# Sums of a weight's four blocks in a fused attention, MoE and GLU kernel: five adding DMAs and two negated copies against four VectorE subtractions

## The chip, the cores and the metric

The kernel runs on one core of a Trainium2 chip. The metric is the device time of one launch in microseconds, as the median of several runs. The engines are TensorE (PE, with its weight loads shown apart as PEld), VectorE (DVE), ScalarE (ACT), GpSimd (POOL) and SyncE (SP); each works through its own list of instructions in the order in which the program wrote them, and waits where an instruction needs something that another engine or a DMA has not finished.

## What is computed

Block-causal attention, then a mixture of eight experts over its output, then a gated linear unit. Cut to what matters:

```python
attn = softmax(mask(q @ k.T / sqrt(64))) @ v          # 4 x 8 heads, 576 positions
x = attn as (2304, 512)
P = eight rounds of row and column normalising of exp(x @ w_gate)
x = sum over e of P[:, e] * (relu(x @ w1[e]) @ w2[e])  # 8 experts, 512 -> 1024 -> 512
g = x @ w_gate2
y = (g * sigmoid(g) * (x @ w_val)) @ w_out             # 512 -> 1536 -> 512
```

## The kernel before

Every matrix product is done at float32 precision with float16 operands: a float32 matrix is scaled by a power of two and cut into a high and a low float16 half, and a product is three float16 products. On top of that a 512 x 512 weight W is cut into four blocks, W11, W12, W21 and W22, and a product uses seven products of block sums in place of eight (a Strassen-Winograd scheme). A weight therefore has to be turned into seven operands: W11, W21, W22, and the sums T1 = W12 - W11, T3 = W22 - W12, T2 = W22 - T1 and T4 = W21 - T2, up to signs. Each operand takes ACT one instruction for its high half (line 173, `split_later`) and DVE one for its low half (line 174); in the code `up(o, src)` issues the first and `low(o)` the second.

The expert weights come as 16 units of 512 hidden columns, each with two weights (w1 and w2). A unit is 63 slots of work of TensorE: five blocks of tokens (four of 256 columns, one of 128), seven operand products each (`products_in`, line 543), with the second product of the unit before (`products_out`, line 651) woven in. A bank of PSUM that `products_in` has filled must be emptied by ACT (lines 560, 568, 572, 779) or by DVE's adds (lines 565, 574, 580) before TensorE gets it again. While TensorE works through unit u, a background list prepares unit u+1's two weights, and, spread over 13 of the units, converts the three GLU weights from float64 words. `Background.step` takes a task from the list (a light one may bring a first task of the next weight along), at most twice a slot, so as to have the list done by slot 58. The maxima of a weight's blocks (`mx`, line 376) come first, then its scale (`end`), and then `sum_tasks`, lines 284 to 345, which is what the change rewrites. 39 weights go through `sum_tasks`: 30 expert weights and 9 pieces of GLU weights (gate, value and output, three each). A unit during which a GLU piece goes through it has three weights to sum in place of two.

In `sum_tasks` before, the sums are made in place in the float32 blocks b[r][c] by `add`: a DMA issued from POOL's queue with accumulation, SBUF to SBUF, 256 KB. So that adding will do, W12 and W21 have been negated in place by ACT (`minus`, line 348), called from `mx` for the expert weights and from `first` (line 494) for the GLU pieces. The last two of the five adds need the result of an earlier one. The low halves are written in the step after the high half, and three empty steps (`gap`) stand among the tasks.

The names in the profile: `wr` are an expert weight's float32 blocks, `w` its operands; `f_g`, `f_v`, `f_o` the blocks of a GLU piece, `gg`, `gv`, `go` their operands; `abc_m_a`, `abc_m_b`, `abc_m_c` the three PSUM banks of `products_in`; `m_t` sums that are taken out of them; `ev` results of the second product, added into `acc` by another DMA with accumulation from POOL's queue (line 1433).

Of the kernel before, what the change touches and what calls it, by code (L numbers as in the profile page):

```python
# [13 lines left out]
AF = mybir.ActivationFunctionType  # L14
ALU = mybir.AluOpType
# [10 lines left out]
W11, W21, W22, T4, T1, T2, T3 = range(7)  # L26
# [4 lines left out]
def attention_moe_glu_kernel(  # L31
# [21 lines left out]
    nc = tc.nc  # L53
# [166 lines left out]
    places = Places(0)  # L220
# [63 lines left out]
    def sum_tasks(b, sp, name, flip):  # L284

        los = {}

        def add(o, x):
            nc.gpsimd.dma_start(o, x, accum_op=ALU.add)  # L292

        def up(o, src, minus=False):
            los[o] = sp(o, src, minus)

        def low(o, *gone):
            los.pop(o)()
            places.give(*gone)

        def t0():
            up(W11, b[0][0])

        def t1():
            low(W11)
            add(b[0][0], b[0][1])
            up(W21, b[1][0], True)

        def t2():
            low(W21)  # L310
            add(b[1][0], b[1][1])
            up(W22, b[1][1])

        def t3():
            low(W22)
            add(b[0][1], b[1][1])

        def t5():
            up(T1, b[0][0], True)
            add(b[1][0], b[0][0])  # L320

        def t6():
            low(T1)
            add(b[1][1], b[0][0])

        def t8():
            up(T3, b[0][1])

        def t9():
            low(T3, b[0][1])  # L330
            up(T4, b[1][0], True)
            places.give(b[0][0])

        def t10():
            low(T4, b[1][0])
            up(T2, b[1][1], flip)

        gap = (0, None, 0)
        return (
            [(1, t0, 0), (1, t1), (1, t2), (0, t3)]  # L340
            + [gap] * 1
            + [(1, t5, 0), (0, t6)]
            + [gap] * 2
            + [(1, t8, 0), (1, t9), (1, t10), (0, lambda: low(T2, b[1][1]))]
        )

    def minus(x):
        nc.scalar.activation(x, x, AF.Copy, scale=-1.0)

    units, made = {}, set()  # L350

    def expert_items(u):
# [8 lines left out]
        for i, W in enumerate((W1, W2)):  # L361
            g = {"b": [[None, None], [None, None]]}
# [9 lines left out]
                        nc.sync.dma_start(b, src.rearrange("(k p) f -> p k f", p=P))  # L372
                g["mx"] = small.tile([P, 4], F32, tag="wmx", name=f"wmx_{u}_{i}")

            def mx(k, g=g, sums=i == 0 or u >= 2):
                nc.vector.tensor_reduce(
                    g["mx"][:, k : k + 1], g["b"][k // 2][k % 2], axis=AX.XY, op=ALU.max, apply_absolute_value=True
                )
                if sums and k > 1:
                    minus(g["b"][(k - 1) // 2][(k - 1) % 2])  # L380

            def begin(g=g, i=i):
                m1 = small.tile([P, 1], F32, tag="wm1", name=f"wm1_{u}_{i}")
# [35 lines left out]
    def glu_items(name, src, rawp):  # L419
# [5 lines left out]
        g = {}  # L425
# [11 lines left out]
        def mx(b, r, c):  # L437
            k = 2 * r + c
            if k == 0:
                g["mx"] = small.tile([P, 4], F32, tag="wmx", name=f"gmx_{name}")  # L440
            nc.vector.tensor_reduce(
                g["mx"][:, k : k + 1], b[r][c], axis=AX.XY, op=ALU.max, apply_absolute_value=True
            )
# [14 lines left out]
        def exponent(cur, b, t, r, c):  # L458
            b[r][c] = places.take(f"f_{name}_{t}_{r}{c}", F32, main=False)
            cur["f"] = b[r][c].rearrange("p k w -> p (k w)")  # L460
            nc.scalar.activation(cur["f"], cur["high"], AF.Copy, scale=2.0**-112)

        def shift(cur):
            fi = cur["f"].bitcast(I32)
            nc.vector.tensor_single_scalar(fi, fi, 3, op=ALU.logical_shift_left)

        def sign(cur):
            fi, hi = cur["f"].bitcast(I32), cur["high"].bitcast(I32)
            nc.vector.scalar_tensor_tensor(fi, hi, -(2**31), fi, op0=ALU.bitwise_and, op1=ALU.bitwise_or)
# [16 lines left out]
        for t, r, c in quads:  # L486
            if (r, c) == (0, 0):
                b = [[None, None], [None, None]]
            cur = {}

            def last(cur=cur, b=b, r=r, c=c):
                mx(b, r, c)

            def first(cur=cur, b=b, q=(t, r, c)):
                exponent(cur, b, *q)
                if q[1:] == (1, 0):
                    minus(b[0][1])
                elif q[1:] == (1, 1):
                    minus(b[1][0])

            tasks = [(1, first, 0)]
            tasks += [(0, lambda cur=cur: (shift(cur), sign(cur))), (0, lambda cur=cur: mantissa(cur)), (0, last, 2)]
            if (r, c) == (1, 1):
                tasks[-1] = (0, lambda last=last, t=t: (last(), begin(t)))
                tasks += [(0, None, 0), (lambda force: across_made(g["r"])(force), lambda t=t: end(t))]
                tasks += sum_tasks(b, lambda o, src, minus=False, t=t: sp(t, o, src, minus), f"g{name}_{t}", name == "o")
            items.append((0, lambda cur=cur, q=(t, r, c): load(cur, *q), tasks))
# [1237 lines left out]
```

## Time and profile before

| | |
|---|---|
| median of 3 runs | 2194.89 us (2191.09 to 2196.18) |
| the profiled execution | 2203.99 us, span 2202.2 us |
| adds of line 292 | 195 of 256 KB |
| adds of line 1433 | 351 of 256 KB |

The profiled execution lies 0.4% above the median of the other runs. Its stages: attention, with the first two units beside it, up to about 390 us; the units up to about 1790 us; then the GLU. Views are read like this. A row of a table by stretch gives the stretch, its length, then busy microseconds of PE, PEld, DVE, ACT and POOL with the number of instructions, the granted TensorE clock (1.00 is 2.4 GHz, 0.5 is 1.2 GHz), the share of time in which DMA engines were busy, and GB/s; the stretches here run from one unit's first weighting on DVE (line 1412) to the next unit's. A row of waits gives who waited for whom, the sum in us, how often, and the longest. A row of the order of time gives the start, the length, the engine, what it did, and in brackets how long the engine had been idle and what ended that. A row of instructions by line ends with count, busy us and the mean in ns.

### The profile page before, as it was taken

To read this page: it belongs to the slowest core of one execution; us is meant where nothing else is said; L and a number is where in the kernel's file an instruction comes from. 1 tells how busy PE (TensorE), PEld (TensorE's weight loads), DVE (VectorE), ACT (ScalarE), POOL (GpSimd) and SP (SyncE) were. 2 spreads that over 40 slices of the span, in tenths; PEclk is the share of its full clock that TensorE was granted. 3 is DMA by queue.
4 is the path that set the end of the run, shared out by engine and by line. 5 is a ranking of instruction groups with operands and counts; after the bars stand their busy time and mean duration, and the time that the engine had idled before them with its cause. 6 is when DMAs were issued, how large, how long until landed. Compare 5 with 4: busy or idle time off the path is not lost.

```text
span 2202.2 us, 47643 instructions
## 1 busy us (share of the span) xinstructions
PE 2001.1 (91%) x18378; PEld 1696.4 (77%) x18378; DVE 1596.5 (72%) x3583; ACT 1366.3 (62%) x2901; POOL 708.0 (32%) x1003
## 2 busy tenths in 40 slices
PE   6789899799989999898998988999888988999997
PEld 3356667688877888777887877888777887888887
DVE  6887774677777787776876767777776787666766
ACT  5666665467676677666776666677666556544442
POOL 4544343203333343333433333343333122100000
PEclk8889999899999999999999999999999999999999
DMA  6343331527887888878888797878879110210211
GB/s 170 104 121 96 106 88 48 148 54 149 173 183 151 171 158 171 185 144 174 157 167 178 145 182 146 176 148 161 186 146 202 40 45 1 57 46 17 62 40 49
DMA packets 180787, 272.22 MB, mean 124 GB/s; under 512 B 18512, under 2 KB 72784, under 8 KB 180560
## 3 DMA queue, kind: packets, MB, share of 16 engines
q0 software_dynamic: 78624, 143.17, 38.5%
q1 hardware_dynamic: 101936, 126.01, 18.7%
q8 instruction: 144, 2.36, 0.4%
q14 instruction: 83, 0.68, 0.1%
HBM read 90.98 MB, written 24.38 MB: 52 GB/s over the span
## 4 chain that ended last, share of the span: by engine, by line
PE 38%; DMA 17%; DVE 12%; issue 8%; ACT 6%; POOL 2%; POOLq 0%; ACTq 0%; DVEq 0%; SPq 0%
DMA wr<-wr 9%; PE abc_m_b L543 7%; PE m_o_b L651 6%; PE m_o_ac L651 5%; PE abc_m_c L543 3%; PE abc_v_b L543 3%; PE m_go_b L651 3%; PE abc_g_b L543 3%; PE m_go_ac L651 2%; PE abc_m_a L543 2%; DMA f_v<-f_v 2%; DMA f_g<-f_g 2%; DVE m_t L710 1%; DVE m_h L183 1%; PE abc_v_c L543 1%
## 5 line engine op out<-in xcount | busy, mean ns | idle before, releaser
L543 PEld LDWEIGHTS <-w 128*128 128x128 f16 x6720 | 620.0, 100 | 185.0 <-issue 111.4
L651 PEld LDWEIGHTS <-m_h 128*128 128x128 f16 x5292 | 521.0, 99 | 77.2 <-issue 11.6
L543 PE MATMUL abc_m_b<-xs,w 128*128 128x256 f16 (+1 forms) x3840 | 490.7, 269 | 71.5 <-DVE m_t L565 33.0
L1433 POOL DMA_DIRECT2D acc<-ev x351 | 340.4, 1098 | 549.7 <-ACT ev L1440 447.9
L651 PE MATMUL m_o_b<-w,m_h 128*128 128x256 f16 x3024 | 407.1, 274 | 5.9 <-ACT ev L1440 5.6
L651 PE MATMUL m_o_ac<-w,m_h 128*128 128x256 f16 x2268 | 320.7, 279 | 3.1 <-ACT ev L1440 3.1
L543 PE MATMUL abc_m_c<-xs,w 128*128 128x256 f16 (+1 forms) x1920 | 235.7, 267 | 22.9 <-ACT m_r L779 21.0
L173 ACT ACTIVATE w<-wr,ws 128x512 f16<-128x512 f32 x210 | 149.4, 720 | 123.1 <-DMA wr<-wr 109.0
L174 DVE SCALAR_TENSOR_TENSOR w<-wr,ws,w 128x512 f16<-128x512 f32 x210 | 156.9, 752 | 94.4 <-ACT w L173 94.1
L292 POOL DMA_DIRECT2D wr<-wr x150 | 147.5, 990 | 228.1 <-DMA wr<-wr 57.2
L1440 ACT ACTIVATE ev<-m_o_b,pe 128x256 f32<-128x256 f32 x351 | 161.6, 475 | 58.1 <-PE m_o_b L651 53.1
L183 DVE TENSOR_TENSOR m_h<-m_t,m_h 128x512 f16<-128x512 f32 (+1 forms) x210 | 132.9, 634 | 35.0 <-ACT m_h L689 34.8
L1440 ACT ACTIVATE ev<-m_o_ac,pe 128x256 f32<-128x256 f32 (+1 forms) x234 | 134.3, 579 | 36.9 <-PE m_o_ac L651 35.8
L682 ACT ACTIVATE m_h<-m_t 128x512 f16<-128x512 f32 (+1 forms) x210 | 120.5, 582 | 36.1 <-DVE m_t L580 18.5
L689 ACT CAST m_h<-m_t 128x512 f16<-128x512 f32 (+1 forms) x210 | 122.0, 581 | 16.7 <-DVE m_t L710 16.4
L686 DVE SCALAR_TENSOR_TENSOR m_h<-m_t,m_h 128x512 f16<-128x512 f32 (+1 forms) x210 | 131.1, 633 | 1.1 <-ACT m_h L682 0.7
L543 PEld LDWEIGHTS <-gg_w 128*128 128x128 f16 x1260 | 114.2, 98 | 21.4 <-issue 9.3
L1002 POOL TENSOR_SCALAR e<-e,r 128x64 f32<-128x64 f32 (+2 forms) x144 | 78.9, 555 | 159.8 <-DVE r L997 100.6
L651 PEld LDWEIGHTS <-g_h 128*128 128x128 f16 x1134 | 111.8, 99 | 19.6 <-issue 5.4
L543 PEld LDWEIGHTS <-gv_w 128*128 128x128 f16 x1260 | 114.4, 98 | 13.3 <-issue 1.2
L543 PE MATMUL abc_m_a<-xs,w 128*128 128x256 f16 (+1 forms) x960 | 119.3, 265 | 0.0
L691 POOL TENSOR_TENSOR g_h<-g_t,g_h 128x512 f16<-128x512 f32 (+1 forms) x15 | 16.0, 1069 | 250.8 <-ACT g_h L689 250.8
(319 smaller groups left out, 3454.8 us busy)
## 6 DMA issues: line engine op xcount, KB each, us to landing
acc<-ev POOLq DMA_DIRECT2D x351, 256.0 KB, 5.3
wr<-wr POOLq DMA_DIRECT2D x150, 256.0 KB, 4.0
wr<-in_w_dram SPq DMA_DIRECT2D x128, 256.0 KB, 4.7
st<-hl SPq DMA_DIRECT2D x48, 144.0 KB, 3.6
raw_g<-in_w_gate_dram SPq DMA_DIRECT2D x12, 512.0 KB, 5.1
raw_v<-in_w_val_dram SPq DMA_DIRECT2D x12, 512.0 KB, 5.4
raw_o<-in_w_out_dram SPq DMA_DIRECT2D x12, 512.0 KB, 4.8
scr_g<-gg SPq DMA_DIRECT2D x21, 256.0 KB, 3.6
```

The lines of the kernel that those rows point to most:

```text
L173: nc.scalar.activation(hi, src, AF.Copy, scale=s)
L174: return lambda: nc.vector.scalar_tensor_tensor(lo, src, s, hi, op0=ALU.mult, op1=ALU.subtract)
L183: nc.vector.tensor_sub(lo, src, hi)
L292: nc.gpsimd.dma_start(o, x, accum_op=ALU.add)
L543: nc.tensor.matmul(ps[:, f], W[o][:, sh, k, f * P : (f + 1) * P], xs[:, o, mh, k, c0 : c0 + n], start=x not in begun, stop=True, skip_grou ...
L651: nc.tensor.matmul(ps, h[o][:, sh, k, ii * P : (ii + 1) * P], W[o][:, mh, k], start=o in (X11, X12) and k == 0 and j == 0, stop=True, skip ...
L682: nc.scalar.activation(hi, src, AF.Relu)
L686: nc.vector.scalar_tensor_tensor(lo, src, 0.0, hi, op0=ALU.max, op1=ALU.subtract)
L689: nc.scalar.copy(hi, src)
L1002: nc.gpsimd.tensor_scalar(et[c][:, :n], et[c][:, :n], g["r"][:, c : c + 1], 1.0, op0=ALU.mult, op1=ALU.mult)
L1433: nc.gpsimd.dma_start(acc[:, x], e, accum_op=ALU.add)
L1440: nc.scalar.activation(e[:, cols], ps, AF.Copy, scale=p)
```

## The change

The five adds and two negations a weight become four subtractions by DVE, in place, and the order of the steps is written anew: each low half now comes two steps after its high half in place of one, no empty steps are left, the tasks of a weight's sums go from 13 to 11, and the order of T2 and T4 is swapped.

```diff
-        def add(o, x):
-            nc.gpsimd.dma_start(o, x, accum_op=ALU.add)
+        def less(o, x, y):
+            nc.vector.tensor_sub(o, x, y)
 
         def up(o, src, minus=False):
             los[o] = sp(o, src, minus)
@@ -298,54 +298,41 @@
             los.pop(o)()
             places.give(*gone)
 
-        def t0():
-            up(W11, b[0][0])
-
-        def t1():
+        def t2():
             low(W11)
-            add(b[0][0], b[0][1])
-            up(W21, b[1][0], True)
-
-        def t2():
+            less(b[0][0], b[0][1], b[0][0])
+
+        def t3():
+            up(W22, b[1][1])
             low(W21)
-            add(b[1][0], b[1][1])
-            up(W22, b[1][1])
-
-        def t3():
+            less(b[0][1], b[1][1], b[0][1])
+
+        def t5():
             low(W22)
-            add(b[0][1], b[1][1])
-
-        def t5():
-            up(T1, b[0][0], True)
-            add(b[1][0], b[0][0])
+            less(b[1][1], b[1][1], b[0][0])
 
         def t6():
-            low(T1)
-            add(b[1][1], b[0][0])
+            up(T3, b[0][1])
+            low(T1, b[0][0])
+            less(b[1][0], b[1][0], b[1][1])
 
         def t8():
-            up(T3, b[0][1])
-
-        def t9():
+            up(T4, b[1][0])
             low(T3, b[0][1])
-            up(T4, b[1][0], True)
-            places.give(b[0][0])
-
-        def t10():
-            low(T4, b[1][0])
-            up(T2, b[1][1], flip)
-
-        gap = (0, None, 0)
-        return (
-            [(1, t0, 0), (1, t1), (1, t2), (0, t3)]
-            + [gap] * 1
-            + [(1, t5, 0), (0, t6)]
-            + [gap] * 2
-            + [(1, t8, 0), (1, t9), (1, t10), (0, lambda: low(T2, b[1][1]))]
-        )
-
-    def minus(x):
-        nc.scalar.activation(x, x, AF.Copy, scale=-1.0)
+
+        return [
+            (1, lambda: up(W11, b[0][0]), 0),
+            (1, lambda: up(W21, b[1][0]), 0),
+            (0, t2),
+            (1, t3),
+            (1, lambda: up(T1, b[0][0]), 0),
+            (0, t5),
+            (1, t6),
+            (1, lambda: up(T2, b[1][1], flip), 0),
+            (1, t8),
+            (0, lambda: low(T2, b[1][1])),
+            (0, lambda: low(T4, b[1][0])),
+        ]
...
-            def mx(k, g=g, sums=i == 0 or u >= 2):
+            def mx(k, g=g):
-                if sums and k > 1:
-                    minus(g["b"][(k - 1) // 2][(k - 1) % 2])
-                if q[1:] == (1, 0):
-                    minus(b[0][1])
-                elif q[1:] == (1, 1):
-                    minus(b[1][0])
```

How it moves instructions, at the second piece of the gate weight (its operands are gg_1_0 to gg_1_6, in the order W11, W21, W22, T4, T1, T2, T3; its blocks f_g_1_00 to f_g_1_11), which is summed during unit 4. DVE before, around the add that empties bank b of block 3 (m4_3_t6):

```order
L174 SCALAR_TENSOR_TENSOR gg_1_6_9902<-f_g_1_01_9070,gs_g_1_9709,gg_1_6_9902 128x512
L174 SCALAR_TENSOR_TENSOR gg_1_3_9937<-f_g_1_10_9506,gs_g_1_9709,gg_1_3_9937 128x512
L565 TENSOR_TENSOR m4_3_t6_9966<-m4_3_t4_9832,abc_m4_3_b_9761 128x512
L686 SCALAR_TENSOR_TENSOR m4_3_h0_9945<-m4_3_t1_9925,m4_3_h0_9945 128x512
L174 SCALAR_TENSOR_TENSOR gg_1_5_9958<-f_g_1_11_9593,gs_g_1_9709,gg_1_5_9958 128x512
```

DVE after, at the same place (line 546 is what was line 565):

```order
L174 SCALAR_TENSOR_TENSOR gg_1_2_9776<-f_g_1_11_9575,gs_g_1_9712,gg_1_2_9776 128x512
L292 TENSOR_TENSOR f_g_1_11_9575<-f_g_1_11_9575,f_g_1_00_8470 128x512
L174 SCALAR_TENSOR_TENSOR gg_1_4_9810<-f_g_1_00_8470,gs_g_1_9712,gg_1_4_9810 128x512
L292 TENSOR_TENSOR f_g_1_10_9489<-f_g_1_10_9489,f_g_1_11_9575 128x512
L174 SCALAR_TENSOR_TENSOR gg_1_6_9849<-f_g_1_01_9043,gs_g_1_9712,gg_1_6_9849 128x512
L174 SCALAR_TENSOR_TENSOR gg_1_5_9867<-f_g_1_11_9575,gs_g_1_9712,gg_1_5_9867 128x512
L546 TENSOR_TENSOR m4_3_t6_9916<-m4_3_t4_9787,abc_m4_3_b_9719 128x512
```

Two subtractions have come in, and six instructions of the weight now stand in a row ahead of the add that empties the bank. ACT before, the same stretch:

```order
L568 COPY m4_3_t5_9878<-abc_m4_3_b_9761 128x512
L1440 ACTIVATE ev4_2_4_0_9844<-m_o4_2_0_b_9837,pe_4_9248 128x256
L173 ACTIVATE gg_1_6_9902<-f_g_1_01_9070,gs_g_1_9709 128x512
L572 COPY m4_3_t1_9925<-abc_m4_3_a_9787 128x512
L1440 ACTIVATE ev4_2_5_0_9853<-m_o4_2_1_b_9846,pe_4_9248 128x256
L173 ACTIVATE gg_1_3_9937<-f_g_1_10_9506,gs_g_1_9709 128x512
L682 ACTIVATE m4_3_h0_9945<-m4_3_t1_9925 128x512
```

ACT after:

```order
L173 ACTIVATE gg_1_4_9810<-f_g_1_00_8470,gs_g_1_9712 128x512
L549 COPY m4_3_t5_9840<-abc_m4_3_b_9719 128x512
L173 ACTIVATE gg_1_6_9849<-f_g_1_01_9043,gs_g_1_9712 128x512
L1421 ACTIVATE ev4_2_4_0_9799<-m_o4_2_0_b_9792,pe_4_9219 128x256
L173 ACTIVATE gg_1_5_9867<-f_g_1_11_9575,gs_g_1_9712 128x512
L553 COPY m4_3_t1_9875<-abc_m4_3_a_9745 128x512
L1421 ACTIVATE ev4_2_5_0_9808<-m_o4_2_1_b_9801,pe_4_9219 128x256
L173 ACTIVATE gg_1_3_9887<-f_g_1_10_9489,gs_g_1_9712 128x512
```

The high halves of T1, T2 and T4 now come after DVE's subtractions, and no longer after a DMA.

## Rows read from the trace of the kernel before

**Rows 1.** The page: TensorE and the other engines over the whole span.

```profile
PE 2001.1 (91%) x18378; PEld 1696.4 (77%) x18378; DVE 1596.5 (72%) x3583; ACT 1366.3 (62%) x2901; POOL 708.0 (32%) x1003
```

**Rows 2.** The table by stretch, unit by unit, five of thirteen units and the sum.

```profile
481.61:569.59 87.98, 83.69 (x798) 74.26 (x796) 67.08 (x138) 70.26 (x141) 32.94 (x38) 1.00 0.76 146
...
763.09:847.27 84.18, 83.54 (x806) 75.15 (x806) 67.27 (x139) 63.98 (x129) 32.88 (x38) 1.00 0.82 157
...
941.11:1041.13 100.02, 88.77 (x813) 77.50 (x811) 72.25 (x150) 66.29 (x135) 37.87 (x43) 0.97 0.83 166
1041.13:1125.67 84.54, 83.68 (x806) 75.15 (x806) 67.33 (x139) 64.11 (x129) 32.91 (x38) 1.00 0.82 158
...
1426.89:1514.05 87.16, 85.14 (x806) 76.05 (x806) 67.35 (x139) 64.20 (x129) 32.94 (x38) 0.98 0.78 151
...
sum 1229.30, PE 1127.59 PEld 990.39 DVE 909.85 ACT 853.10 POOL 458.67; mean PE 86.74 PEld 76.18 DVE 69.99 ACT 65.62 POOL 35.28
```

**Rows 3.** The same table for the adds of line 292 alone, two units.

```profile
763.09:847.27 84.18, 9.71 (x11) 1.00 0.82 157
...
941.11:1041.13 100.02, 15.34 (x15) 0.97 0.83 166
```

**Rows 4.** Waits over the whole span that end with an add or follow one.

```profile
ACT w L173 <- DMA wr<-wr: 109.0, 69, 4.1
...
DVE w L174 <- ACT w L173: 94.1, 78, 4.5
...
ACT go L173 <- DMA f_o<-f_o: 20.1, 10, 4.9
ACT gg L173 <- DMA f_g<-f_g: 20.0, 11, 4.7
...
ACT gv L173 <- DMA f_v<-f_v: 18.6, 9, 4.7
```

**Rows 5.** Waits of TensorE between 410 and 1760 us, the two largest.

```profile
PE abc_m_b L543 <- DVE m_t L565: 26.6, 13, 4.5
PE abc_m_b L543 <- ACT abc_m_a L560: 23.7, 10, 5.7
```

**Rows 6.** The order of time in unit 4, at a stop of TensorE.

```profile
716.55 0.82 PE L651 MATMUL m_o_b<-w,m_h 128*128 128x256 f16 x6
719.69 0.72 ACT L173 ACTIVATE gg<-f_g,gs_g 128x512 f16<-128x512 f32 x1 [4.75 <-DMA f_g<-f_g]
...
720.44 0.75 DVE L174 SCALAR_TENSOR_TENSOR gg<-f_g,gs_g,gg 128x512 f16<-128x512 f32 x1 [5.57 <-ACT gg L173]
...
721.11 0.68 DVE L565 TENSOR_TENSOR m_t<-m_t,abc_m_b 128x512 f32<-128x512 f32 x1
...
721.85 1.44 PE L543 MATMUL abc_m_b<-xs,w 128*128 128x256 f16 x6 [4.48 <-DVE m_t L565]
```

**Rows 7.** Instructions by line, shapes apart: float32 sums in SBUF, and the negations.

```profile
L348 ACT ACTIVATE wr<-wr 128x512 f32<-128x512 f32 x60 | 37.6, 626 | 15.6 <-DVE wmx L376 14.0 <-DMA wr<-in_w_dram 1.6
...
L712 DVE TENSOR_TENSOR g_a<-g_t,g_a 128x512 f32<-128x512 f32 x12 | 8.7, 726 | 0.4
...
L712 DVE TENSOR_TENSOR g_t<-g_t,g_t 128x512 f32<-128x512 f32 x12 | 8.2, 684 | 0.0
```

**Rows 8.** The table by stretch for the two stretches with the busiest VectorE.

```profile
1596.00:1614.00 18.00, 18.00 (x168) 16.16 (x166) 16.52 (x36) 12.65 (x26) 4.68 (x7) 1.00 0.71 138
1254.00:1272.00 18.00, 16.18 (x141) 13.89 (x142) 16.99 (x45) 12.25 (x25) 7.37 (x9) 1.00 0.78 155
```

**Rows 9.** DMA issues: count, KB each, median us from issue to landing.

```profile
wr<-wr POOLq DMA_DIRECT2D x150, 256.0 KB, 4.0
...
f_v<-f_v POOLq DMA_DIRECT2D x15, 256.0 KB, 6.6
```

**Rows 10.** VectorE's waits over the whole span, at the add that empties bank b.

```profile
DVE m_t L565 <- PE abc_m_b L543: 21.3, 24, 2.0
```

**Rows 11.** Instructions by line: that add, all shapes.

```profile
L565 DVE TENSOR_TENSOR m_t<-m_t,abc_m_b 128x512 f32<-128x512 f32 (+1 forms) x80 | 50.3, 629 | 24.6 <-PE abc_m_b L543 21.3 <-ACT ev L1440 3.2
```

## The prediction

> **What bounds the kernel now.** I read the page first: TensorE is busy for 91% of the span, VectorE for 72%, ScalarE for 62% [rows 1]. A change off TensorE can then bring at most what TensorE stands still, and what it works at the lower clock. The second view, the table by stretch cut at the units, says where that is. The 13 units between 481.61 and 1710.91 us are of two kinds [rows 2]. Four of them (87.98, 84.18, 84.54 and 87.16 us) have two weights to sum: 343.86 us together, 85.97 each, and TensorE is busy 336.05 us of it. The other nine have a GLU piece as a third weight. Taken as the sum less the four, they hold 1229.30 - 343.86 = 885.44 us, 98.38 each, and TensorE is busy 1127.59 - 336.05 = 791.54 us, 87.95 each. So a unit with three sums is 12.4 us longer than one with two, for the same products. 8.5 us of this is TensorE standing still (10.4 against 1.95 us) and 3.9 us is the same matmuls taking longer: the granted clock is 0.97 in the one such unit shown, and 0.98 to 1.00 in the four others.
>
> What does TensorE wait for there? Its largest waits are for banks that DVE or ACT have not emptied: 26.6 us for DVE's add and 23.7 us for ACT's copy [rows 5]. Those engines have waits of their own, in front of the weights' operands: ACT stands 109.0 us for the adds of expert weights and 20.1, 20.0 and 18.6 us for those of the GLU pieces, 167.7 us in all, and DVE stands 94.1 us for the expert operands that ACT then brings late [rows 4]. The order of time at one stop ties these together [rows 6]: ACT is idle for 4.75 us until an add of f_g lands at 719.69; DVE is idle for 5.57 us behind it; DVE's next instruction is the add that empties bank b; TensorE, done with its last matmuls after 716.55, has stood 4.48 us when it starts at 721.85, and its next six matmuls then span 1.44 us where the six before span 0.82, as the lower of the clock's two levels, 1.2 GHz, would have it. An in-order engine that waits for a DMA holds up all that is queued behind it, the banks too.
>
> That the adds do this only where three weights are summed is seen as well: the unit of 84.18 us has 11 adds in it and no stop to speak of, the one of 100.02 us has 15 [rows 3].
>
> **The change part by part.**
>
> *The adds go* (195 DMAs), and with them the waits above. ACT's instruction for T1, T2 or T4 now waits for a subtraction of DVE that was written two or more steps earlier. If that cured everything that sets the nine units apart, they would fall to 85.97 us: 9 x 12.42 = 111.8 us. This is the upper end for the first term, apart from the four lighter units, where the distance to the best of them is 4 x (85.97 - 84.18) = 7.2 us more. I do not count these 7.2.
>
> *Subtractions come in on DVE*: 39 x 4 = 156, on 128 x 512 float32 in SBUF. The nearest rows are the GLU's own sums of that shape and kind, 684 to 726 ns [rows 7]; I take the lower, 0.684 us; the upper would add 0.042 us to each of 140, 6 us, inside the range. A unit with two weights gets 8 (5.5 us), one with three gets 12 (8.2 us). DVE is busy 67.3 us in the former (269.03 us in four) and (909.85 - 269.03) / 9 = 71.2 us in the latter, so it comes to 72.7 and 79.4 us. In a unit of 85.97 us that is 85% and 92%. Do such shares leave TensorE alone? The two stretches with the busiest DVE answer it from both sides [rows 8]: at 16.52 of 18 us (92%) TensorE is busy all 18.00, at 16.99 of 18 (94%) it loses 1.82 us, a tenth. Below that I count nothing. For the nine units I take the middle, 5% of 84.18 us or 4.2 us each: 38 us. Nothing and a tenth (8.4 each, 76 us) are the ends. I do not take the favourable row alone because of what the order shows: six instructions of the weight, four low halves and two subtractions, now stand in a row ahead of the add that empties bank b, where two stood; at about 0.7 us each that is some 4 us of DVE's list without a bank emptied. What hides it is DVE's freedom elsewhere in the unit, and if that is used up TensorE waits at that add.
>
> *The negations go*: 78 on ACT at 0.626 us [rows 7], 49 us of ACT's time. ACT's share is not what bounds a unit (its waits are), and what it gives is inside the first term: nothing more is counted. POOL's list loses the 195 issues, and nothing waits for POOL there but the other adds, those into acc, which land sooner or at the same time: nothing.
>
> *The steps.* 11 tasks in place of 13 a weight, four of them light in place of six, so the number of heavier steps stays at seven and a unit's list is spread as before. Nothing.
>
> *Before the first of the 13 units* four weights are summed, during attention and just after it. Their 16 subtractions cost 16 x 0.684 = 10.9 us if every one stood on the path; their adds cost at most what one of the nine units loses to them, 12.4 us, on the evidence of rows where only a third weight makes them hurt. I take nothing, with these two ends. After 1711 us nothing is changed.
>
> *The sum*: -111.8 + 38 = -74 us. The profiled execution is 2203.99 us long and lies 9.1 us above the median; the difference is taken off the median: 2194.89 - 74 = 2121 us.
>
> **The rivals.**
>
> *VectorE becomes the bound.* The subtractions are not hidden but stand in the path, all of them: 9 x 8.2 + 4 x 5.5 + 10.9 = 107 us against 111.8. That gives 2190 us, no change. If half of them do, 2137. For it: 92% leaves no room for a wait. Against it: the 92% row with TensorE at 100% [rows 8], and that DVE loses its own idle time behind ACT (94.1 us for expert weights alone, [rows 4]). The Trainium skill speaks for this rival: its page "Perfetto Trace Analysis", section "Optimizing Scalar/DVE Operations", says that if VectorE is saturated, moving some of its work to ScalarE or GpSimd may make sense, and the change does the reverse. By that rule the time would be this rival's; at 72% over the span the trace shows a VectorE that is not saturated, at 92% of a unit it would be close. I give it 8 in 100.
>
> *The adds were hidden.* As in the units with two weights, they cost nothing anywhere, and the nine units are long because of the GLU piece's other work. Then nothing is gained and little lost: 2195 us, or up to 2204 with a quarter of DVE's 38 us. Against it: the stop of [rows 6] begins with an add. The rows give an add 4.0 us from issue to landing, 6.6 us for f_v [rows 9], and ACT comes for the sum before that. The Trainium skill ("DMA: Bandwidth & Descriptors", section "Anatomy of one DMA — SWDGE (gpsimd) path") has 2.0 us plus bytes at 436 GB/s for one such DMA; an estimate from it is 2.6 us for 256 KB, and by that an add would mostly have landed when ACT comes and this rival would hold. The trace differs and decides. 5 in 100.
>
> *Slower: the bank-emptying add comes late at every sum.* Mechanism: a low half and a subtraction go in back to back just ahead of line 565's add, TensorE stops for each subtraction (0.684 us), and restarts at 1.2 GHz, which costs 0.62 us over its next six matmuls (1.44 less 0.82, [rows 6]): 1.30 us for each of the 140 subtractions in the 13 units, 182 us, against 111.8 gained. It decides from 86 of the 140 on; at 80% of them it is 2229 us. For it: the order. Against it: DVE came to that add before TensorE was done in only 24 cases [rows 10] of the 80 adds that line 565 makes for the units [rows 11], and TensorE waited for it in 13 [rows 5]; in most of the others DVE was later than TensorE with no harm, so there is slack between. 6 in 100.
>
> That the change does not do what it says is ruled out by the order: 156 new rows on DVE, 195 fewer on POOL.
>
> **How the numbers follow.** The forecast, nine units near 90 us, has 81 in 100. Its own range is 2076 (no cost on DVE, all 7.2 us of the light units too) to 2170 (a tenth lost and 10.9 us before). The range for all cases, 2080 to 2165, leaves out the tails of the forecast (5 in 100 together), the full form of the first rival and the other two (15), and holds the first rival's half form at 2137. What can be told from no change is 0.2%, 4.4 us. Faster by more than this: the forecast and the first rival short of its full form, 0.88. Within it: that full form and the second, 0.06. Slower: the third, 0.06.
>
> **What would show it.** In the table by stretch the nine long units should come to 87 to 93 us with the clock at 0.98 or above, the four others should stay at 84 to 88. ACT's waits in front of line 173 for wr and f_g, f_v, f_o are gone, and those that take their place, for DVE's subtractions, are below 40 us in all. DVE's wait for ACT at line 174 falls from 94.1 to below 40 us. A subtraction takes 0.68 to 0.73 us. DVE's busy time rises by 90 to 107 us, to about 1700. TensorE's waits for DVE's add of bank b stay at some 25 us, and those for ACT fall by more than half. I am wrong if the nine units keep their 98 us (the adds were not the cause), if the lighter units grow past 88 us with TensorE waiting for DVE (the list is too full), or if ACT's waits for DVE take the place of those for the DMAs.

## The result

The changed kernel takes 2119.65 us (median of 4 runs, 2117.28 to 2121.61) against 2193.26 us (4 runs, 2191.09 to 2196.18): a ratio of 0.9665, with an interval of 0.9649 to 0.968. The forecast was 2121 us. That the sum came out right doesn't say that its terms were, so both stand below: first the trace by the prediction's own list, then what each term measured on its own.

The page of the changed kernel, its line of busy times, answers to [rows 1]:

```profile
PE 1968.2 (93%) x18378; PEld 1683.5 (79%) x18378; DVE 1685.4 (80%) x3739; ACT 1335.6 (63%) x2823; POOL 537.0 (25%) x808
```

VectorE's work rose by 88.9 us, POOL's fell by 171.0, and TensorE works 32.9 us less for the same 18378 matmuls: it spends less time at the lower clock (the granted clock, averaged over the span, is 0.976 where it was 0.960). The table by stretch of the changed kernel, from unit to unit as in [rows 2]; four units with two sums, one with three, and the sum of thirteen:

```profile
476.05:562.28 86.23, 82.12 (x787) 73.31 (x786) 70.43 (x144) 66.93 (x133) 23.45 (x27) 1.00 0.59 118
...
744.00:827.82 83.82, 82.50 (x795) 74.07 (x795) 70.07 (x144) 60.44 (x122) 23.24 (x27) 1.00 0.62 123
...
916.52:1009.78 93.26, 86.78 (x813) 76.56 (x811) 79.52 (x161) 64.40 (x129) 23.24 (x27) 0.98 0.64 137
1009.78:1094.18 84.40, 82.51 (x795) 74.08 (x795) 70.07 (x145) 60.45 (x122) 23.30 (x27) 1.00 0.60 121
...
1276.42:1361.43 85.01, 83.57 (x805) 75.01 (x805) 71.69 (x147) 61.62 (x124) 23.29 (x27) 1.00 0.61 122
...
sum 1156.72, PE 1101.21 PEld 980.24 DVE 990.24 ACT 827.83 POOL 302.63; mean PE 84.71 PEld 75.40 DVE 76.17 ACT 63.68 POOL 23.28
```

The four light units add up to 339.46 us, 84.87 each. That leaves 817.26 us for the nine long ones, 90.81 each: the unit that took 100.02 us takes 93.26. The 13 units lost 72.6 us.

The waits of the changed kernel over the whole span, those that answer to [rows 4] (who waited for whom, sum in us, how often, longest):

```profile
DVE w L174 <- ACT w L173: 7.6, 9, 1.2
...
ACT gg L173 <- DVE f_g L292: 2.3, 5, 0.6
ACT w L173 <- DVE wr L292: 1.8, 4, 0.8
...
ACT gv L173 <- DVE f_v L292: 1.6, 4, 0.6
...
ACT go L173 <- DVE f_o L292: 1.2, 4, 0.4
```

ACT's 167.7 us in front of the sums are 6.9 us, and VectorE's 94.1 us behind ACT are 7.6. What TensorE still waits for, between 400 and 1760 us, the two largest as in [rows 5]:

```profile
PE abc_m_b L524 <- DVE m_t L546: 28.7, 18, 2.4
PE m_o_b L632 <- ACT ev L1421: 16.7, 18, 1.9
```

The first sum is as large as before, but its stops are others: no longer a few of up to 4.5 us behind a DMA, but 18 of at most 2.4 us. Of the 18, 14 with 25.3 us of the sum stand at the last block of a unit, whose matmuls have 128 columns; the other four are of some 0.85 us each. The order of time at one of the 14, in the changed kernel:

```profile
620.26 0.69 DVE L292 TENSOR_TENSOR wr<-wr,wr 128x512 f32<-128x512 f32 x1
...
620.86 0.69 DVE L183 TENSOR_TENSOR m_h<-m_t,m_h 128x512 f16<-128x512 f32 x1
...
621.46 0.75 DVE L174 SCALAR_TENSOR_TENSOR w<-wr,ws,w 128x512 f16<-128x512 f32 x1
...
622.24 0.69 DVE L292 TENSOR_TENSOR wr<-wr,wr 128x512 f32<-128x512 f32 x1
622.85 0.41 DVE L546 TENSOR_TENSOR m_t<-m_t,abc_m_b 128x256 f32<-128x256 f32 x1
...
623.32 1.44 PE L524 MATMUL abc_m_b<-xs,w 128*128 128x128 f16 x12 [2.37 <-DVE m_t L546]
```

A low half and a subtraction stand directly ahead of the add that empties bank b, TensorE stands 2.37 us, and then its 12 matmuls span 1.44 us where 12 of the same took 0.83 us a little earlier (line 524 at 618.14): the granted clock is 0.50 there, the lower of its two levels. This is the mechanism of the third rival, at one or two places in a unit and not at every sum. Its restart at the lower clock isn't the rule either: after 7 of the 18 stops the granted clock fell to 0.50 for about 3 us, and after 11 it stayed at 1.00, as after this one, which is as long as the stop above:

```profile
890.15 0.83 PE L524 MATMUL abc_m_b<-xs,w 128*128 128x128 f16 x12 [2.38 <-DVE m_t L546]
```

### The profile page after: what moved, and what is told of

Read it like the earlier page. It is cut to its first block, busy times and chain, and to the rows that moved or that the text cites. A ratio compares the mean times of both kernels' runs of the same rounds, so it can differ in the third digit from the quotient of the medians.

```text
span 2119.8 us, 47322 instructions
## 1 busy us (share of the span) xinstructions
PE 1968.2 (93%) x18378; PEld 1683.5 (79%) x18378; DVE 1685.4 (80%) x3739; ACT 1335.6 (63%) x2823; POOL 537.0 (25%) x808
## 4 chain that ended last, share of the span: by engine, by line
PE 51%; DVE 21%; issue 4%; ACT 3%; DMA 2%; POOL 0%; SPq 0%; DVEq 0%; ACTq 0%; POOLq 0%
PE abc_m_b L524 10%; PE m_o_b L632 10%; PE m_o_ac L632 7%; PE abc_m_c L524 5%; PE abc_m_a L524 3%; PE m_go_b L632 3%; PE abc_g_b L524 3%; DVE m_t L691 3%; PE abc_v_b L524 3%; DVE m_h L183 2%; PE m_go_ac L632 2%; DVE w L174 2%; DVE m_h L667 2%; PE abc_g_c L524 1%; PE abc_v_c L524 1%
## 5 line engine op out<-in xcount | busy, mean ns | idle before, releaser
L632 PEld LDWEIGHTS <-m_h 128*128 128x128 f16 x5292 | 516.4, 98 | 84.2 <-issue 20.2
L1414 POOL DMA_DIRECT2D acc<-ev x351 | 302.8, 874 | 945.9 <-ACT ev L1421 758.5
L524 PE MATMUL abc_m_b<-xs,w 128*128 128x256 f16 (+1 forms) x3840 | 483.1, 266 | 38.2 <-DVE m_t L546 33.6
L632 PE MATMUL m_o_b<-w,m_h 128*128 128x256 f16 x3024 | 408.2, 274 | 19.1 <-ACT ev L1421 16.7
L632 PE MATMUL m_o_ac<-w,m_h 128*128 128x256 f16 x2268 | 310.8, 273 | 0.0
L983 POOL TENSOR_SCALAR e<-e,r 128x64 f32<-128x64 f32 (+2 forms) x144 | 78.1, 548 | 168.5 <-DVE r L978 106.9
L587 PEld LDWEIGHTS <-m_h 128*128 128x128 f16 x864 | 83.7, 99 | 16.9 <-issue 7.0
L363 DVE TENSOR_REDUCE wmx<-wr 128x1 f32<-128x512 f32 x128 | 86.2, 679 | 10.3 <-DMA wr<-in_w_dram 9.9
```

Of the source, the lines that this page charges most:

```text
L363: nc.vector.tensor_reduce(g["mx"][:, k : k + 1], g["b"][k // 2][k % 2], axis=AX.XY, op=ALU.max, apply_absolute_value=True)
L524: nc.tensor.matmul(ps[:, f], W[o][:, sh, k, f * P : (f + 1) * P], xs[:, o, mh, k, c0 : c0 + n], start=x not in begun, stop=True, skip_grou ...
L587: nc.tensor.matmul(p[:, c * TB : (c + 1) * TB], h[t, r][:, sh, k, ii * P : (ii + 1) * P], W[r, c][:, mh, k], start=c == 0 and j == 0, stop ...
L632: nc.tensor.matmul(ps, h[o][:, sh, k, ii * P : (ii + 1) * P], W[o][:, mh, k], start=o in (X11, X12) and k == 0 and j == 0, stop=True, skip ...
L1414: nc.gpsimd.dma_start(acc[:, x], e, accum_op=ALU.add)
```

## The experiments

Each ratio is to the kernel before, run on the same chip. The medians of before differ by up to 5 us between the four groups of runs, so across groups I compare ratios and turn them into us with 2193.3.

### Which half of the change: the adder or the steps

*Old steps, adds on VectorE.* The steps, gaps and negations of before:

```diff
-            nc.gpsimd.dma_start(o, x, accum_op=ALU.add)
+            nc.vector.tensor_add(o, o, x)
```

> The kernel before with its steps, its gaps and its two negations a weight left as they are; only the five adds a weight are made by VectorE in place (195 additions of 128x512 float32) in place of the DMAs. Theory of the waits (ACT, in order, stood until an add had landed, and the banks behind it): most of the gain is here, 2115 to 2145 us, with ACT's waits in front of line 173 down from 167.7 us to below 60. Theory of the steps (the two steps between high and low half and the lost gaps made the gain): 2180 to 2200 us.

Measured 2152.63 us, ratio 0.9809 (0.9777 to 0.9842). VectorE in place of the DMA is a gain by itself, of 42 us, in the old steps and with one operation a weight more than the change has. It missed both ranges and left 32 us of the gain open. The waits did what their theory had said (below 60 us): no row of ACT's waits at line 173 names a sum any more. What is left of TensorE's waits has another cause: it still stands 30.3 us, 20 times, for the add that empties bank b.

*New steps, sums by DMA.* The changed kernel with four adding DMAs a weight (156 of 256 KB) and the negations in place of the subtractions:

```diff
-            nc.vector.tensor_sub(o, x, y)
+            nc.gpsimd.dma_start(o, x, accum_op=ALU.add)
...
-            less(b[0][0], b[0][1], b[0][0])
+            add(b[0][0], b[0][1])
...
-            (1, lambda: up(W21, b[1][0]), 0),
+            (1, lambda: up(W21, b[1][0], True), 0),
```

> [...] Theory of the waits: ACT still comes for T1, T2, T3 and T4 before the adds have landed, 2165 to 2200 us. Theory of the steps: 2115 to 2135 us.

Measured 2353.7 us, ratio 1.0718 (1.0684 to 1.0752): far above both. Its waits over the whole span say why:

```profile
ACT w L173 <- DMA wr<-wr: 251.0, 114, 5.7
POOL wr L292 <- DMA wr<-wr: 160.8, 56, 4.6
```

ACT's wait of [rows 4] went from 109.0 to 251.0 us with fewer DMAs. The new steps bring ACT to a sum soon after its add was issued; the old ones had gaps there. So the new steps suit an adder that is done in 0.69 us; with the DMAs they are a loss.

*The change for a part of the weights.* The function of before is kept as `sum_tasks_dma` beside the new one, and is called, with the negations that it needs, for the GLU pieces:

```diff
-                tasks += sum_tasks(b, lambda o, src, minus=False, t=t: sp(t, o, src, minus), f"g{name}_{t}", name == "o")
+                tasks += sum_tasks_dma(b, lambda o, src, minus=False, t=t: sp(t, o, src, minus), f"g{name}_{t}", name == "o")
```

or, in a second kernel, for the 30 expert weights:

```diff
-                tasks += sum_tasks(g["b"], sp, f"w{i}_{u}", i == 1)
+                tasks += sum_tasks_dma(g["b"], sp, f"w{i}_{u}", i == 1)
```

> The change made for the 30 expert weights alone; the 9 GLU pieces keep their 45 adding DMAs, their negations and their steps. Theory of the waits: of the stops of TensorE above 1 us that end with an add, some 39 of 65 us follow the GLU pieces' adds, so about two fifths of the 73.6 us are gained: 2155 to 2172 us, with ACT's waits for f_g, f_v and f_o still at 50 to 60 us. Theory of the traffic (fewer bytes moved by the DMA engines is what helps): 150 of 195 adds are gone, so three quarters are gained, 2130 to 2143 us.

> The change made for the 9 GLU pieces alone; the 30 expert weights keep their 150 adding DMAs. Theory of the waits: about three fifths are gained, 2140 to 2158 us, and the nine long units fall to some 93 us. Theory of the traffic: 45 of 195 adds are gone, a quarter is gained, 2170 to 2180 us.

Measured 2154.98 us, ratio 0.9809 (0.9782 to 0.9837), for the expert weights alone, and 2136.67 us, 0.9732 (0.9705 to 0.9759), for the GLU pieces alone. The pieces have 45 of the 195 adds and bring 59 us, the expert weights have 150 and bring 42. The theory that each add costs by its traffic falls. The theory of the waits names the right half, but both results lie just below its ranges. They fit the reading that it's the third weight in a unit, whose adds come when the unit is full, as in [rows 3]. The two gains add to 101 us and the whole is 73. Why they don't add up is not shown: one half cured may take part of the other's stops along, or VectorE's operations, of which the whole change brings 156 and the halves 120 and 36, may cost more the more there are, as the next experiments find.

### What an operation on VectorE or ScalarE costs there

*Two copies a weight on ScalarE*, where the negations had been, in the changed kernel:

```diff
+    def same(x):
+        nc.scalar.activation(x, x, AF.Copy, scale=1.0)
```

> The changed kernel with two copies a weight by ScalarE (in place, unchanged values) where the kernel before had its two negations: 78 more ScalarE operations of 0.63 us, 49 us of ScalarE's busy time; steps and subtractions stay the changed kernel's. It asks which part of the 33 us between the five adds by VectorE in the old steps (2152.6 us) and the change (2119.65 us) the negations are. Negations cost nothing (ScalarE is busy for 63% of the span, my term of zero): 2117 to 2124 us. Negations stand in the way, because the copy lies between the last bank's emptying and the next operation of ScalarE: all of the 33 us, 2145 to 2153 us; half of it, about 2135 us.

Measured 2123.36 us, ratio 0.9661 (0.9629 to 0.9694), the same as the change. 78 operations and 38.6 us of ScalarE's work cost nothing that can be told: the zero for the negations holds.

*The same, and one more VectorE operation a weight*, so that the counts are those of the old steps:

```diff
+            nc.vector.tensor_tensor(b[1][1], b[1][1], b[1][1], op=ALU.max)
```

> The kernel with the two copies a weight, and one more VectorE operation a weight (a maximum of a block with itself, the size and operand count of a subtraction, values unchanged): 195 VectorE operations and 78 ScalarE operations as in the old steps with adds by VectorE (2152.6 us), so that between these two only the order and places of the steps are left. If the counts of operations are the 33 us: 2145 to 2157 us, VectorE busy about 1710 us. If the steps are: 2120 to 2130 us. At the price of my sum (4.2 us for 6.9 us of VectorE work a unit, so 0.6 of the added 25 us) the added VectorE operation alone is worth 15 us: 2132 to 2140 us.

Measured 2150.09 us, ratio 0.9795 (0.9763 to 0.9827): the old steps' 0.9809 again. So with five operations a weight the steps make no difference that can be told, and the 32 us left open above go with the count. The added 39 cost 26.7 us on the same chip, 0.69 us each: an operation's whole duration. The fifth stands directly behind a subtraction here, which it doesn't in the old steps, so its number isn't told apart from its place.

*An operation more ahead of each subtraction*:

```diff
+            nc.vector.tensor_tensor(o, o, o, op=ALU.max)
             nc.vector.tensor_sub(o, x, y)
```

> The changed kernel with a second VectorE operation ahead of each of the four subtractions (a maximum of the block with itself, values unchanged): 156 more operations of 0.60 to 0.69 us, 94 to 108 us more VectorE busy time, 84% of the span. It measures the price of VectorE time by itself, which my sum set at 4.2 us for 6.9 us of work (0.6 of it). By that price: 2175 to 2185 us. VectorE as the bound (every added us is lost, the second rival): 2210 to 2230 us. VectorE's idle time hides it: 2120 to 2135 us. The wait of TensorE for VectorE at a block's middle add, 28.7 us in the changed kernel, should grow with the loss.

Measured 2230.48 us, ratio 1.016 (1.013 to 1.019): 0.0495 above the change, 109 us for 156 operations, 0.70 us each. The price in my sum (2175 to 2185 us) is refuted for these; the full price holds, at the upper end of its range. Yet VectorE isn't full over a unit. A light unit of this kernel in the table by stretch:

```profile
778.86:869.45 90.59, 84.54 (x796) 74.88 (x795) 75.62 (x152) 60.65 (x122) 23.27 (x27) 0.98 0.58 114
```

TensorE's two largest waits in this kernel, between 400 and 1760 us:

```profile
PE abc_m_b L525 <- DVE m_t L547: 69.1, 21, 4.9
PE m_o_b L633 <- ACT ev L1422: 43.9, 26, 3.5
```

VectorE is busy for 75.62 of 90.59 us, 83%, and the unit is still 6.77 us longer than in the changed kernel (83.82) for eight operations. TensorE's waits for the two engines that empty its banks grew by 40.4 and 27.2 us, and its busy time by 38.7 (2006.9 us on the page): an operation here costs by delaying what empties a bank, and not by filling VectorE's time over the unit. It does so on ScalarE too, which copies `ev` out of the other banks: its waits for the subtractions grew from 6.9 to 39.1 us, a sign that the prediction had named and that the change itself doesn't show.

*Subtractions alone, left out*, and *the adds alone, left out*. In the changed kernel:

```diff
-            nc.vector.tensor_sub(o, x, y)
+            pass
```

> The changed kernel without its four subtractions a weight (the sums are left out, the blocks are spilled as they are; nothing else moves): 156 VectorE operations and some 100 us of its work less. It asks whether the 0.71 us an operation that the 156 added operations of twice_subtracted cost also holds for the 156 that the change brought. At that price: 2120 - 110 = 2005 to 2015 us. At the price in my sum (4.2 us in each of 13 units): about 2065 us. If the subtractions lie in idle time: 2100 us or more.

and in the kernel before:

```diff
-            nc.gpsimd.dma_start(o, x, accum_op=ALU.add)
+            pass
```

> The kernel before without its five adding DMAs a weight (the sums are left out; the two negations, the steps and the gaps stay): it measures what the DMAs and the waits for them cost by themselves, the first term of my sum (111.8 us over the nine long units). By that term: 2193 - 112 = 2075 to 2085 us. If the gain of the change is the difference of two larger amounts, a full price for VectorE's subtractions (about 110 us) and the DMAs' whole cost: 2193 - 184 = about 2010 us, near the changed kernel without its sums. If the adds were hidden: 2185 us or more.

Measured 2056.68 us, ratio 0.9389 (0.9361 to 0.9417), and 2078.48 us, ratio 0.9486 (0.9464 to 0.9508). My new theory (both amounts near 110 and 184 us) falls here, and the prediction's terms come nearer: the adds cost 113 us, the 156 subtractions 61 us, 0.39 each. The full price is that of operations on top of these. The sum over the 13 units in the table by stretch, first of the changed kernel without subtractions:

```profile
sum 1103.79, PE 1086.58 PEld 974.22 DVE 904.62 ACT 821.95 POOL 302.26; mean PE 83.58 PEld 74.94 DVE 69.59 ACT 63.23 POOL 23.25
```

and then of the kernel before without adds:

```profile
sum 1121.06, PE 1092.89 PEld 976.47 DVE 907.93 ACT 855.44 POOL 302.32; mean PE 84.07 PEld 75.11 DVE 69.84 ACT 65.80 POOL 23.26
```

*VectorE's work taken away.* The scaled identities of the maxima by ScalarE:

```diff
-            nc.vector.tensor_scalar_mul(d[:, i], ident, mx[:, i : i + 1])
+            nc.scalar.activation(d[:, i], ident, AF.Copy, scale=mx[:, i : i + 1])
```

> The changed kernel with the small scaled identities of the maxima (128x128, 0.286 us on VectorE, 34 of them in the units and some 40 around them) made by ScalarE: it takes VectorE work away in the units, 34 x 0.286 = 9.7 us, and gives ScalarE as much. If every us of VectorE in the units is a us of the kernel: 2107 to 2112 us. If the price of VectorE time sets in only above the present load: 2117 to 2122 us. If the scaled identity comes later through ScalarE's queue and TensorE or the next scale waits for it: 2122 to 2135 us.

Measured 2119.02 us, ratio 0.9669 (0.965 to 0.9688): the same as the change, though VectorE's busy time fell from 1685.4 to 1664.5 us, 9.3 us of it in the 13 units. Of these 9.3 none that can be told came back. ScalarE got as much work, so a gain and a loss that cancel are not ruled out; its row as a cause of TensorE's stops hardly moved (16.0 us in place of 16.7).

*One subtraction of four by GpSimd*:

```diff
-            less(b[0][1], b[1][1], b[0][1])
+            nc.gpsimd.tensor_tensor(b[0][1], b[1][1], b[0][1], op=ALU.subtract)
```

> The changed kernel with the second of the four subtractions of a weight by GpSimd, from the same two blocks in place: 39 operations leave VectorE (27 us of its busy time). GpSimd is idle in three quarters of a unit. If the stops at the last block of each sum (28.7 us of TensorE's waits for VectorE) come from VectorE's load, 2100 to 2115 us; if GpSimd takes several us for it, or slows VectorE beside it, so that the block's spill on ScalarE waits as it did for the DMAs: 2130 to 2170 us, with a row of ScalarE's waits for GpSimd.

Measured 2139.6 us, ratio 0.975 (0.972 to 0.9779), 19 us slower than the change. GpSimd's instruction in this kernel by its line, with the least, the median and the largest duration in ns:

```profile
L308 POOL TENSOR_TENSOR wr<-wr,wr x30: 1265/1598/1709, 35.2 to 1614.9; 128x512 f32<-128x512 f32 x30
```

VectorE's low halves in this kernel, on the page (the changed kernel has 746 and 633 ns there):

```profile
L174 DVE SCALAR_TENSOR_TENSOR w<-wr,ws,w 128x512 f16<-128x512 f32 x210 | 161.7, 771 | 7.6 <-ACT w L173 7.6
L667 DVE SCALAR_TENSOR_TENSOR m_h<-m_t,m_h 128x512 f16<-128x512 f32 (+1 forms) x210 | 134.9, 656 | 1.6 <-ACT m_h L663 1.6
```

VectorE lost 39 operations and is busy for 9.5 us more (1694.9 on the page). The row of ScalarE's waits for GpSimd that I had named is 0.8 us: the loss goes with VectorE's other work being longer, not with a late sum. The means hide how: the middle one of the low halves is as long as before (744 ns, in the changed kernel 745), and a few are long, each beside a subtraction on GpSimd. The order of time at one:

```profile
477.71 1.27 POOL L308 TENSOR_TENSOR wr<-wr,wr 128x512 f32<-128x512 f32 x1 [2.82 <-DVE wr L292]
477.88 1.64 DVE L174 SCALAR_TENSOR_TENSOR w<-wr,ws,w 128x512 f16<-128x512 f32 x1
```

Between 440 and 1740 us 35 of VectorE's instructions take over 0.95 us, and 34 of them overlap with one of GpSimd's 35 subtractions there. The longest takes 2.44 us in place of 0.69 (line 183 at 610.78), and a subtraction of 1.59 us on GpSimd lies wholly within it.

### The subtractions apart from the low halves

If the price is one of place, the same instructions spread out should cost less. Here each subtraction is a step of its own, in the changed kernel; the cut shows two of the four, and the others are split likewise:

```diff
-            (0, t2),
-            (1, t3),
+            (0, lambda: low(W11)),
+            (0, t2),
+            (1, lambda: (up(W22, b[1][1]), low(W21))),
+            (0, t3),
```

> The changed kernel with each subtraction as a step of its own, apart from the low half that the change had put into the same step (15 steps a weight in place of 11, the same instructions in the same order within a weight). The four subtractions a weight cost 63 us (2119.65 against 2056.7 us without them), 0.40 us each, and 156 more behind them cost 0.71 us each. It asks whether that price comes from where they stand (a low half and a subtraction in a row, 1.4 us, ahead of the add that empties a bank) or from VectorE's load. By the place: fewer instructions in a row ahead of that add, TensorE's waits for it fall below 28.7 us, and the kernel comes to 2095 to 2112 us, faster than both. By the load: the same work, 2117 to 2125 us. If more steps in a unit only push the same work to the unit's end, where the list has to be finished: 2125 to 2145 us.

Measured 2103.24 us (5 runs), ratio 0.9593 (0.958 to 0.9606): 16 us faster than the change and the fastest kernel here that leaves nothing out, with as many instructions of VectorE and ScalarE. TensorE's largest wait in this kernel, between 400 and 1750 us:

```profile
PE abc_m_b L522 <- DVE m_t L544: 14.0, 15, 1.3
```

The order of time in this kernel at the last block of the unit of which the stop of 2.37 us was shown:

```profile
612.45 0.69 DVE L292 TENSOR_TENSOR wr<-wr,wr 128x512 f32<-128x512 f32 x1
...
614.33 0.41 DVE L544 TENSOR_TENSOR m_t<-m_t,abc_m_b 128x256 f32<-128x256 f32 x1
...
614.79 0.83 PE L522 MATMUL abc_m_b<-xs,w 128*128 128x128 f16 x12 [0.65 <-DVE m_t L544]
...
615.26 0.68 DVE L292 TENSOR_TENSOR wr<-wr,wr 128x512 f32<-128x512 f32 x1
```

The two subtractions now lie on either side of the bank's add, the stop is 0.65 us and the 12 matmuls take 0.83 us. VectorE hardly pauses around either stop (it is busy for 10.70 of 10.80 us there in the changed kernel and for 8.37 of 8.40 in this one), so what differs here is the order in its list. TensorE's waits for that add fell from 28.7 to 14.0 us, and after each of these 15 stops the granted clock is 1.00. Of the 20.0 us between the two spans (2119.8 and 2099.8), 11.2 lie in the 13 units (1145.50 us in all) and 9.5 ahead of the first of them (it begins at 466.60 us, not 476.05). Fifteen steps in place of eleven also move work among the slots and units: the four light units are longer than in the change (348.93 in place of 339.46 us), the nine others shorter (796.57 in place of 817.26), and the fourth light unit is the eleventh of the 13 where it was the tenth. This was not told apart from the place within a weight.

## Why the prediction was right, and where not

*Its reading of the profile.* That ACT, VectorE and TensorE were held one behind the other by the adds is borne out: without the DMAs the nine long units take 86.85 us each (781.61 of the 1121.06), close to the 85.97 that the four light ones had given as their floor. The rival that the adds were hidden falls with the 113 us. The Trainium skill's formula ("DMA: Bandwidth & Descriptors", section "Anatomy of one DMA — SWDGE (gpsimd) path"), by which I had estimated 2.6 us for an add, would have had it hold; the measured 4.0 and 6.6 us of [rows 9] decided rightly.

*Its list.* The nine long units were to take 87 to 93 us: they take 90.81 on average, two lie a little above (93.26 and 93.15), and the clock is 0.98 or above in all. The light ones were to stay at 84 to 88 and take 83.82 to 86.23. ACT's waits for the subtractions (below 40 us) are 6.9, and VectorE's for ACT (below 40) 7.6. A subtraction (0.68 to 0.73 us) takes 694 ns for the expert blocks and 688 or 689 for the pieces. VectorE's busy time was to rise by 90 to 107 us and rose by 88.9, just below: two VectorE instructions in a row start 0.60 us apart while each is shown as 0.69 long, and what overlaps counts once. TensorE's wait for the add of bank b (some 25 us) is 28.7. Its waits for ACT were to fall by more than half: the copy of bank a, 23.7 us in [rows 5], fell to 1.7, and all of its rows for ACT together from 70.0 to 29.7, although the one for `ev` grew from 5.6 to 16.7.

*Its terms.* The trace's stretches give each of them; the numbers are differences of the three tables by stretch and of the points at which the first unit begins (481.61 before, 469.00 without adds, 464.10 without subtractions, 476.05 after):

| term | in the sum, us | measured, us |
|---|---|---|
| adds gone, nine long units | -111.8 | -103.8 |
| adds gone, four light units | 0 | -4.4 |
| adds gone, before the first unit | 0 (0 to -12.4) | -12.6 |
| subtractions, nine long units | +38 (0 to 76) | +46.4 |
| subtractions, four light units | 0 | +6.5 |
| subtractions, before the first unit | 0 (0 to +10.9) | +12.0 |
| steps and negations, units and before | 0 | -22.2 |

These add to -78.1; the other 4.3 of the 82.4 us between the spans lie behind the last unit. Of the 9.1 us by which the profiled execution of before was long, part may stand in the three terms of the adds, which add to 120.8 us where the ratio gives 113.

By the ratios, in this order of taking the change apart, 113 us are gained with the adds, 22 with steps and negations (2078.48 less 2056.68, same chip), and 61 are lost with the subtractions: 74 in all. In this order the step that failed is "*The steps.* ... Nothing": without any sums they hold 22 us, where I had counted tasks only. What changes with them in these two traces are VectorE's waits for ACT at line 174, 48.6 us in the old steps and 16.2 in the new, where a low half comes two steps after its high half in place of one. That this makes the 22 us, or how much of it the negations make, wasn't tried apart; with the subtractions in place two copies cost nothing. The second mis-sized term is then the subtractions', 61 us where I had 38; the light units and the start, set at zero, hold 18.5 of it. The two misses, +23 and -22, cancel.

The same runs in another order give another account. With the adds left out 113 us are gained, five sums a weight by VectorE in the old steps lose 71 (0.9809 less 0.9486), the new steps with the same counts gain 3 that can't be told from nothing (0.9795), and the fifth operation and the two copies taken out gain 29 (0.9665). That is -113 for the adds, -3 for the steps and +42 for four subtractions, against -111.8, 0 and +38 in the sum. So the steps are worth 22 us where no sums stand in VectorE's list and nothing that can be told where five a weight do. The terms depend on each other, and it isn't settled whether the sum came out by two errors or by none. Part of it is luck in either order: the adds' 113 us are near 111.8 although the nine long units, of which that term spoke, gave 103.8 by the stretches, and 17.0 came from the light units and the start, which had been set at zero.

*The price of VectorE's time.* I took a share (5% of a unit) between two stretches with a busy VectorE, [rows 8]. The size was near, the reason wasn't: the runs point to what stands ahead of a bank's add. 9.3 us of other VectorE work, taken out of the units, brought nothing that can be told, eight operations in a light unit at 83% cost 6.77 us, and spreading the same subtractions out gave back 16, with the reservations above. I had seen the place, in the six instructions in a row that the order shows, and used it only to pick a middle value.

*The rivals.* VectorE as the bound, in its full form, would have been 107 us for the subtractions; they cost 61, so in that order its half form was the nearer one, and its price, a whole operation, is what the further ones that were tried paid. The Trainium skill's advice that had spoken for this rival ("Perfetto Trace Analysis", section "Optimizing Scalar/DVE Operations") is to take work off a saturated VectorE. At 80% of the span it isn't saturated here, and taking work off it brought nothing with ScalarE and a loss with GpSimd: ratios 0.9669 and 0.975, against 0.9665. The same section warns that moving work between GpSimd and VectorE might not help because they share an SBUF port, and the longer VectorE instructions beside GpSimd's in that run agree. The third rival, the bank's add late at every sum, held at few places, most of them the last block of a unit: 18 stops and not 140, 28.7 us.

## What to carry to other kernels

A DMA in front of an in-order engine is dear by what that engine would have done next for others, and a unit of work that has one more such chain shows it; comparing units with and without it sized the gain to a tenth. Price an operation on the engine that replaces it by what it stands ahead of (here the add that empties a PSUM bank) and not by the engine's busy share alone, and write operations that needn't stand together into separate steps, so that an urgent one can get between. A sum that comes out right doesn't show that its terms were: leave each half out alone, one run each, and take the change apart in more than one order, since terms that share an engine's list don't simply add.

## What the runs showed of the hardware

- A 128x512 float32 subtraction on GpSimd took 1265 to 1709 ns against 694 on VectorE, and VectorE's instructions that ran beside it were held up: 34 of them took 1.04 to 2.44 us in place of 0.69 to 0.75, while the middle one of 210 low halves took 744 ns, in the changed kernel 745.
- VectorE's instructions of 0.69 us start 0.60 us apart when one follows another, so 156 more of them raised its busy time by 88.9 us and not by 108.
- The granted clock can fall after short stops of TensorE, and the length of the stop alone doesn't decide it: in the changed kernel it fell to 0.50 within the first microsecond after a stop of 0.85 us (at 681.03) and after one of 2.37 (at 623.32), and stayed at 1.00 for the next 5 us after one of 2.38 (at 890.15).
- An adding DMA of 256 KB (of the expert blocks) landed in 4.0 us in the kernel before and 3.3 us in the kernel with 39 fewer of them, and yet ACT's waits for it rose from 109.0 to 251.0 us: the landing time alone says little of what it costs.
